# A gated mix of linear attention and a state-space convolution: how the filter taps reach all partitions, and when they are prepared

## The chip, the cores and the metric

The kernel runs on one core of one Trainium2 chip. A core has a matrix engine (TensorE; PE in the profile, its weight loads PEld), a vector engine (VectorE, DVE), a scalar engine (ScalarE, ACT), a general engine (GpSimd, POOL) and a queue engine that mostly issues transfers (SyncE, SP). The metric is the time of one execution on the device in microseconds (us); the profile adds the span, from the first to the last instruction.

## The reference

For one sequence of 2048 positions with 448 channels the reference computes, cut to its core:

```
q, k, v = split(x @ wqkv)                 # 16 heads of 28 channels
phi(t)  = where(t > 0, t + 1, exp(t)) + 1e-6
kv      = sum over s of phi(k)^T v        # per head; not causal
a       = (phi(q) @ kv / (phi(q) . sum phi(k) + 1e-6)) @ wo
K[d, l] = 2 Re sum_n C[d, n] dt[d] exp(A[d, n] dt[d] l)      # filter taps
b       = causal_convolution(x, K) + x * D_skip
g       = sigmoid(sum(x * gate_w))
out     = g * a + (1 - g) * b
```

A is -exp(log_A_real) + i A_imag, C is C_real + i C_imag, dt is exp(log_dt), with 256 modes for each of the 448 channels.

## The kernel before

Positions are cut into 16 chunks of 128 (`NC`, numbered c), channels into 4 groups of 112 (`J`, `DJ`). Products in full precision are made of rounded parts: an operand is split into a high part (a cast on ScalarE) and a low part (the rest, a subtraction on GpSimd or VectorE; `split_t`, `split_n`, `low`), and each product is three rounds of matmuls.

The order of the work is written out by hand, and each engine runs its own instructions strictly in that order. One turn of the main loop (L476, c from 2 to 13) does this:

- SP issues the load of chunk c + 3 (`load_x`, L200).
- TensorE projects the keys of chunk c + 1 (`project` into PSUM tile "k" or "v1", 11 matmuls, L334). ScalarE (L360, L361, then `k_high`, L366) and VectorE (L362, then `k_low`, two times L372) turn them into features.
- TensorE projects the queries of chunk c (`project` into PSUM tile "q", 11 matmuls). `q_post` makes features of them: ScalarE L380 and L349, VectorE L350 and L353. L353 is the last reader of tile "q". PSUM is full: there is one tile "q", one "k", "v0", "v1" and four sums "g".
- TensorE adds the products of features and positions to the four sums (`do_g`, 11 matmuls, L403).
- ScalarE and GpSimd split chunk c + 2 (`split_t`: L240, L236; `split_n`: L246, L236, and `skip`, L252).

The convolution of this input needs only the first tap of each channel, as a running sum over positions times that tap. `do_v` (L410, L411) multiplies by a triangle of ones, `tri`, for chunks 0 and 1 in turn c = 5 and later for the rest; `v_post` (L415, VectorE) multiplies by the row of taps `near`, which has the 448 taps in every partition; the last row of each product goes by two small transfers into `u` (L418, SP), and GpSimd adds the product to `y` (L423). `gcr` is a second constant, used after the loop.

The generator `s4d_prepare` (from L279) makes the taps and tests that the first tap is enough. `steps(n)` lets it run over n of its pieces: the exponentials before the loop; sums over the modes of channel groups 0 and 1 (L290 and L291 on ScalarE, L292 on VectorE) at the end of c = 2, of groups 2 and 3 at the end of c = 3; thirteen small VectorE instructions on 112 partitions x 4 (L280, L281, L299 to L309) at the end of c = 4; then, in c = 5, between the query projection and `do_g`, the four transposes that spread the result `p0`, 112 x 4, over 128 partitions (L313, TensorE) and the copy from PSUM into `near` (L314, ScalarE):

```
o = ps.tile([P, 512], F32, name="p", tag="v1")
for j in range(J):
    PE.transpose(o[:, j * DJ:(j + 1) * DJ], p0[:, j:j + 1].to_broadcast([DJ, P]), ident[:DJ, :DJ])
ACT.copy(near, o[:, :D])
```

At the end of c = 3, behind the L292 of groups 2 and 3, VectorE also casts `tri` (L511) and `gcr` (L512). The parameters of the convolution, `abc`, are four arrays of 448 KB that lie in space of `pq` which chunks 6 to 15 fill later. They are loaded by four transfers, with the load of chunk 4 behind the first (L230, L200). The output weights `wvo`, 1792 KB, are loaded in turn c = 4 (L482) and first read in turn c = 11 (L531). After the loop come the products with the sums, the normalisation and the output chunk by chunk (`turn`, `attend`, `final_b`).

Of the kernel before, what the change touches and what calls it, by code (L numbers as in the profile page):

```python
# [7 lines left out]
F32 = mybir.dt.float32  # L8
# [7 lines left out]
P = 128  # L16
S = 2048
D = 448
# [3 lines left out]
NC = S // P  # L22
J = 4
DJ = D // J
# [116 lines left out]
def gated_mix_kernel(ctx: ExitStack, tc: tile.TileContext, xin, wq_d, wvo_d, abc_d, ldt_d, dsk_d,  # L141
                     turn_d, cst_d, first_d, gin_d, out):
    nc = tc.nc
    PE, ACT, DVE, POOL, SP = nc.tensor, nc.scalar, nc.vector, nc.gpsimd, nc.sync

    keep = ctx.enter_context(tc.tile_pool(name="keep", bufs=1))
    pq = keep.tile([P, NC, D], F32, name="pq")
# [9 lines left out]
    work = ExitStack()  # L157
# [7 lines left out]
    ident, trir = both[:, 0], both[:, 1]  # L165
    cst = const.tile([P, DJ + RX + 1], F32, name="cst")
    mask, gcat, sel = cst[:DJ, :DJ], cst[:UZ, DJ:DJ + RX], cst[:, DJ + RX:]
    gcr = const.tile([UZ, RX], F32R, name="gcr")
    ones = const.tile([P, P], F32R, name="ones")
    rows = const.tile([P, S], F32, name="rows")  # L170
    near, dsk = (rows[:, i * D:(i + 1) * D] for i in range(2))
# [8 lines left out]
    tri = const.tile([P, P], F32R, name="tri")  # L180
# [3 lines left out]
    xn_p = work.enter_context(tc.tile_pool(name="xn", bufs=7))  # L184
    tp = work.enter_context(tc.tile_pool(name="tp", bufs=2))
    ps = work.enter_context(tc.tile_pool(name="ps", bufs=1, space=PSUM))

    warm = tp.tile([P, 512], mybir.dt.bfloat16, name="warm", tag="e")
    POOL.memset(warm, 1.0)
# [7 lines left out]
    def load_x(c):  # L197
        r = xp.tile([P, XC], F32, name="xr", tag="xr")
        turned[c], plain[c] = r[:, :NAT], r[:, NAT:]
        SP.dma_start(out=r, in_=xin[c])  # L200
# [4 lines left out]
    abc = pf[:DJ, 3 * J * N:7 * J * N].rearrange("p (i j n) -> p i j n", i=4, j=J)  # L205
    wkr = {}
    o = 0
    for part in PARTS:
# [8 lines left out]
        o = e  # L217
# [8 lines left out]
    SP.dma_start(out=dsk, in_=dsk_d.to_broadcast([P, D]))  # L226
    load_x(3)
    SP.dma_start(out=ldt, in_=ldt_d)
    for i in range(4):
        SP.dma_start(out=abc[:, i], in_=abc_d[:, i])  # L230
        if i == 0:
            load_x(4)
    SP.dma_start(out=both, in_=turn_d)

    def low(eng, o, r, h):
        eng.tensor_tensor(out=o, in0=r, in1=h.bitcast(F32), op=ALU.subtract)  # L236

    def split_t(c):
        w = xt[c] = xt_p.tile([P, 2 * NAT], F32R, name="xt", tag="t")
        ACT.copy(w[:, :NAT], turned[c])  # L240
        low(POOL, w[:, NAT:], turned[c], w[:, :NAT])

    def split_n(c):
        r, w = plain[c], xn_p.tile([P, NX], F32R, name="xn", tag="n")
        xn[c] = w
        ACT.copy(w[:, :XC - NAT], r)  # L246
        low(POOL, w[:, XC - NAT:], r[:, :D], w[:, :D])
        if c > 2:
            skip(c)

    def skip(c):
        POOL.tensor_tensor(out=y[:, c], in0=plain[c][:, :D], in1=dsk, op=ALU.mult)  # L252
# [22 lines left out]
    def small():  # L275
        cnt[0] += 1
        return sm[:, cnt[0] - 1]

    def s4d_prepare():  # L279
        tt = lambda eng, o, a, b, op: eng.tensor_tensor(out=o, in0=a, in1=b, op=op)  # L280
        stt = lambda o, a, k, b, op1: DVE.scalar_tensor_tensor(out=o, in0=a, scalar=k, in1=b, op0=ALU.mult, op1=op1)  # L281
        junk = [yf[:DJ, F0 + (i - 2) * 2 * N:F0 + (i - 1) * 2 * N].rearrange("p (i n) -> p i n", i=2) for i in range(2)]
        s0, s1, dt, am, p0, p1, d2, md, b0, b1 = (small() for _ in range(10))
        for j in range(J):
            ACT.activation(abc[:, 0, j], abc[:, 0, j], AF.Exp)
        ACT.activation(dt, ldt, AF.Exp)
        tt(DVE, d2, dt, dt, ALU.mult)
        yield
        for j in range(J):
            ACT.activation(junk[0], abc[:, 0:2, j], AF.Square, accum_out=am[:, j:j + 1])  # L290
            ACT.activation(junk[0][:, 0], abc[:, 2, j], AF.Copy, accum_out=s0[:, j:j + 1])  # L291
            DVE.scalar_tensor_tensor(out=junk[1], in0=abc[:, 2:4, j], scalar=1.0, in1=abc[:, 0:2, j], op0=ALU.mult,  # L292
                                     op1=ALU.mult, accum_out=s1[:, j:j + 1])
            if j % 2:
                yield
        tt(DVE, md, am, d2, ALU.mult)
        stt(p0, s0, 2.0, dt, ALU.mult)
        stt(p1, s1, -2.0, d2, ALU.mult)
        DVE.tensor_scalar(out=md, in0=md, scalar1=SMALL, scalar2=None, op0=ALU.is_le)  # L299
        stt(b0, p0, -1.0, p0, ALU.max)  # L300
        stt(b1, p1, -1.0, p1, ALU.max)
        yield
        DVE.tensor_scalar(out=p0, in0=p0, scalar1=-BIG, scalar2=BIG, op0=ALU.max, op1=ALU.min)
        DVE.scalar_tensor_tensor(out=md, in0=b0, scalar=1.0 / FAR, in1=md, op0=ALU.is_ge, op1=ALU.mult)
        stt(okc, b1, FLAT, b0, ALU.is_le)
        DVE.scalar_tensor_tensor(out=md, in0=b0, scalar=FAR, in1=md, op0=ALU.is_le, op1=ALU.mult)
        tt(DVE, okc, okc, md, ALU.mult)
        tt(DVE, p0, p0, okc, ALU.mult)
        DVE.tensor_reduce(out=oks, in_=okc, op=ALU.add, axis=AX.X)  # L309
        yield  # L310
        o = ps.tile([P, 512], F32, name="p", tag="v1")
        for j in range(J):
            PE.transpose(o[:, j * DJ:(j + 1) * DJ], p0[:, j:j + 1].to_broadcast([DJ, P]), ident[:DJ, :DJ])  # L313
        ACT.copy(near, o[:, :D])  # L314

    def pieces(c, wh, wl, n, tag, last=None):
        o = ps.tile([P, 512], F32, name=tag, tag=tag)
# [20 lines left out]
    def project(*args, **kw):  # L338
        o, run = pieces(*args, **kw)
        run(11)  # L340
        return o
# [15 lines left out]
    def k_feature(c, o):  # L357
        e = tp.tile([P, D], F32, name="e", tag="e")
        pks[c] = o[:, :D]
        ACT.activation(e, pks[c], AF.Relu, scale=-1.0)  # L360
        ACT.activation(e, e, AF.Exp, scale=-1.0)  # L361
        DVE.scalar_tensor_tensor(out=pks[c], in0=pks[c], scalar=1.0, in1=e, op0=ALU.add, op1=ALU.max)  # L362

    def k_high(c):
        pkh[c] = tp.tile([P, 512], F32R, name="pkh", tag="pkh")[:, EDGE:EDGE + D]
        ACT.add(pkh[c], pks[c], 1e-6)  # L366
# [41 lines left out]
    def do_v(c):  # L408
        v = vt[c] = ps.tile([P, 512], F32, name="v", tag="v%d" % (c % 2))
        PE.matmul(v[:, :D], lhsT=tri, rhs=xn[c][:, :D], start=True, stop=False)  # L410
        PE.matmul(v[:, :D], lhsT=tri, rhs=xn[c][:, XC - NAT:], start=False, stop=True)  # L411

    def v_post(c):
        t = tp.tile([P, D], F32, name="t", tag="v0")
        DVE.tensor_tensor(out=t, in0=vt.pop(c)[:, :D], in1=near, op=ALU.mult)  # L415
        if c < NC - 1:
            for k in (c, UL + c):
                SP.dma_start(out=u[k:k + 1], in_=t[P - 1:P])  # L418
            v_add(c, t)
        return t  # L420

    def v_add(c, t):
        POOL.tensor_tensor(out=y[:, c], in0=y[:, c], in1=t, op=ALU.add)  # L423

    prep = s4d_prepare()
    def steps(n):
        for _ in range(n):
            next(prep, None)
# [47 lines left out]
    for c in range(2, NC - 2):  # L476
        if c + 3 < NC:
            load_x(c + 3)
        if c == 2:
            SP.dma_start(out=cst, in_=cst_d)  # L480
        if c == 4:
            SP.dma_start(out=wvo, in_=wvo_d)  # L482
        vs = VS.get(c, ())
        ko = project(c + 1, wkh, wkl, D, "v1" if c in (2, 4) else "k")
        for v in vs[:1]:
            do_v(v)
        split_t(c + 2)
        k_feature(c + 1, ko)
        k_high(c + 1)
        if c > 5:  # L490
            for v in vs[:1]:
                v_post(v)
        k_low(c + 1)
        qo = project(c, wqh, wql, D + 2, "q")
        if c == 5:
            steps(1)
        else:
            for v in vs[1:]:
                do_v(v)
        q_post(c, qo)  # L500
        if c == 10:
            split_n(c + 2)
        if c == 5:
            v_post(0)
        else:
            for v in vs[1:]:
                v_post(v)
        if c < 5:
            steps(2 if c == 4 else 1)
        if c == 3:  # L510
            DVE.tensor_copy(tri, trir)  # L511
            DVE.tensor_copy(gcr, gcat)  # L512
        if c == 7:
            SP.dma_start(out=okr[:, None, :DJ], in_=oks[:, None, :])
        if c == 9:
            DVE.tensor_reduce(out=okr[:, DJ:], in_=okr[:, :DJ], op=ALU.add, axis=AX.X)
            DVE.tensor_copy(okn, okr[:, DJ:])
        do_g(c)
        if c == 5:
            do_v(1)  # L520
        if c < 4:
            skip(c - 1)
        if c != 10:
            split_n(c + 2)
        if c == 5:
            v_post(1)
        for j in {11: (0, 1), 12: (2, 3)}.get(c, ()):
            w = xn_p.tile([P, NX], F32R, name="wo", tag="n")[:DJ, :2 * D].rearrange("p (i d) -> p i d", i=2)
            woh.append(w[:, 0])
            wol.append(w[:, 1])  # L530
            ACT.copy(woh[j], wo[:, j])  # L531
            low(POOL, wol[j], wo[:, j], woh[j])
# [109 lines left out]
    c = NC - 2  # L642
# [294 lines left out]
```

## Time and profile before

| | us |
|---|---|
| median of three runs (lowest, highest) | 174.25 (173.95, 174.47) |
| the profiled execution | 174.06 |
| its span | 172.2 |
| TensorE busy in the span | 167.8 |
| VectorE busy | 113.9 |
| ScalarE busy | 96.0 |
| GpSimd busy | 120.0 |

How to read it: a busy share is an average over the whole span. A group's row names the line, the engine, the operation, what it writes and reads, and its size; then how many there were. In the timeline a row begins with its start and its duration in us, and what stands in brackets is the idle time of that engine just before it and whose work ended that. Successive instructions overlap a little, so a row may start before the row ahead of it has ended. SPq rows are issues of transfers: the transfer itself lands later. The slices of the page cut the span into 40 equal parts of 4.3 us.

### The profile page before, as it was taken

What the parts mean: (1) busy time and instruction counts of PE and PEld (TensorE: products, weight loads), DVE (VectorE), ACT (ScalarE), POOL (GpSimd) and SP (SyncE); (2) the same over time, 40 slices, a digit from 0 to 9 for tenths busy, and PEclk for the clock granted to TensorE, in tenths of its full rate; (3) what the DMA queues carried; (4) which work ended last, traced back from release to release, by engine and by line L of the source; (5) the groups of instructions that cost most, each with busy time, mean ns of one, the idle gap of its engine ahead of it and who ended that gap; (6) DMA issues with size and microseconds to landing.
All of it is one profiled execution on the core that took longest, in us unless ns stands there. A gap on an engine that the chain in (4) does not pass through costs nothing. (4 is left out here: it accounts for less than half of the span.)

```text
span 172.2 us, 2796 instructions
## 1 busy us (share of the span) xinstructions
PE 167.8 (97%) x876; PEld 152.0 (88%) x876; DVE 113.9 (66%) x240; ACT 96.0 (56%) x221; POOL 120.0 (70%) x128
## 2 busy tenths in 40 slices
PE   6999999999999999999999999999999999999992
PEld 2788999999899999999999999999899999999992
DVE  0847737698975483846627346487898998987542
ACT  3688588894256262542727456356574564664541
POOL 6082667877529988696996999529968998892200
PEclk9999999999999999999999999999999999999999
DMA  5989975097003031230404200000031222122213
GB/s 173 415 297 294 268 209 166 0 368 303 4 0 114 11 123 34 95 123 1 122 15 131 106 1 1 0 0 2 7 67 54 107 89 76 62 99 107 108 59 108
DMA packets 7962, 18.60 MB, mean 108 GB/s; under 512 B 2045, under 2 KB 4810, under 8 KB 7818
## 3 DMA queue, kind: packets, MB, share of 16 engines
q1 hardware_dynamic: 7802, 18.30, 32.0%
q8 instruction: 7, 0.11, 0.3%
q10 hardware_dynamic: 144, 0.11, 0.2%
q14 instruction: 9, 0.07, 0.1%
HBM read 14.38 MB, written 3.67 MB: 105 GB/s over the span
## 5 line engine op out<-in xcount | busy, mean ns | idle before, releaser
L629 PE MATMUL a<-wk,th 128*128 128x448 f32 (+1 forms) x170 | 36.4, 360 | 0.0
L403 PE MATMUL g<-pkh,xn 128*128 128x448 f32 x112 | 35.6, 364 | 0.0
L629 PEld LDWEIGHTS a<-wk,th 128*128 128x128 f32 x170 | 29.5, 189 | 1.6
L334 PE MATMUL k<-wk,xt 128*128 128x448 f32 x132 | 29.3, 367 | 0.0
L334 PE MATMUL q<-wqh,xt 128*128 128x450 f32 x120 | 27.5, 366 | 0.0
L362 DVE SCALAR_TENSOR_TENSOR k<-k,e 128x448 f32<-128x448 f32 x12 | 7.6, 632 | 29.4 <-ACT e L361 29.4
L423 POOL TENSOR_TENSOR y<-y,t 128x448 f32<-128x448 f32 x16 | 18.7, 1168 | 11.5 <-DVE t L415 11.5
L334 PEld LDWEIGHTS k<-wk,xt 128*128 128x128 f32 x132 | 24.8, 189 | 2.2 <-DVE wk L236 0.3
L334 PEld LDWEIGHTS q<-wqh,xt 128*128 128x128 f32 x120 | 22.5, 188 | 1.7
L236 POOL TENSOR_TENSOR xn<-xr,xn 128x448 fp32r<-128x448 f32 x16 | 19.4, 1211 | 6.6 <-ACT xn L246 4.5
L403 PE MATMUL g<-pkl,xn 128*128 128x448 f32 x64 | 23.4, 366 | 0.0
L403 PEld LDWEIGHTS g<-pkh,xn 128*128 128x128 f32 x112 | 21.0, 188 | 2.2
L236 POOL TENSOR_TENSOR xt<-xr,xt 128x512 fp32r<-128x512 f32 x14 | 18.2, 1297 | 5.9 <-ACT xt L240 5.9
L360 ACT ACTIVATE e<-k 128x448 f32<-128x448 f32 x12 | 6.5, 544 | 26.9 <-PE k L334 26.9
L542 POOL TENSOR_TENSOR prod<-pq,zb 128x448 f32<-128x448 f32 x16 | 18.6, 1172 | 4.1 <-ACT zb L665 3.0
L252 POOL TENSOR_TENSOR y<-xr,rows 128x448 f32<-128x448 f32 x16 | 18.8, 1175 | 0.0
L567 POOL TENSOR_TENSOR pn<-pq,den 128x336 f32<-128x336 f32 x16 | 12.3, 771 | 5.9 <-ACT den L556 4.1
L634 DVE SCALAR_TENSOR_TENSOR ot<-y,og,a 128x448 f32<-128x448 f32 (+1 forms) x17 | 10.7, 629 | 5.1 <-PE a L629 5.1
L612 DVE TENSOR_TENSOR th<-tr,th 128x512 fp32r<-128x512 f32 x16 | 11.0, 691 | 2.7 <-ACT th L611 2.1
L403 PEld LDWEIGHTS g<-pkl,xn 128*128 128x128 f32 x64 | 11.2, 174 | 1.2 <-DVE pkl L372 0.2
L611 ACT CAST th<-tr 128x512 fp32r<-128x512 f32 x16 | 9.4, 588 | 4.6 <-PE tr L604 4.4
L334 PE MATMUL q<-wql,xt 128*128 128x450 f32 x45 | 11.6, 364 | 0.0
(150 smaller groups left out, 302.3 us busy)
## 6 DMA issues: line engine op xcount, KB each, us to landing
xr<-in SPq DMA_DIRECT2D x15, 512.0 KB, 6.2
out<-ot SPq DMA_DIRECT2D x15, 224.0 KB, 1.9
pq<-in SPq DMA_DIRECT2D x4, 448.0 KB
wvo<-in SPq DMA_DIRECT2D x1, 1792.0 KB
y<-in SPq DMA_DIRECT2D x2, 480.0 KB
y<-in SPq DMA_DIRECT2D x2, 450.0 KB
u<-t SPq DMA_DIRECT2D x30, 1.8 KB, 1.7
y<-in SPq DMA_DIRECT2D x1, 448.0 KB, 4.3
```

The lines of the kernel that those rows point to most:

```text
L236: eng.tensor_tensor(out=o, in0=r, in1=h.bitcast(F32), op=ALU.subtract)
L252: POOL.tensor_tensor(out=y[:, c], in0=plain[c][:, :D], in1=dsk, op=ALU.mult)
L334: PE.matmul(o[:, :n], lhsT=a, rhs=b, start=run.n == 1, stop=not seq)
L362: DVE.scalar_tensor_tensor(out=pks[c], in0=pks[c], scalar=1.0, in1=e, op0=ALU.add, op1=ALU.max)
L403: PE.matmul(g[i][:a.shape[1], :D], lhsT=a, rhs=b, start=c == 0 and n == 0, stop=c == NC - 1 and n == len(seq) - 1)
L423: POOL.tensor_tensor(out=y[:, c], in0=y[:, c], in1=t, op=ALU.add)
L542: POOL.tensor_tensor(out=pd[c], in0=pq[:, c], in1=zb, op=ALU.mult)
L567: POOL.tensor_tensor(out=n[:, :3, :DJ].rearrange("p j (h d) -> p j h d", h=4), in0=a, in1=r[:, :H - 4].rearrange("p (j h) -> p j h", j=3)[ ...
L611: ACT.copy(h, ov)
L612: DVE.tensor_tensor(out=l, in0=ov, in1=h.bitcast(F32), op=ALU.subtract)
L629: PE.matmul(a[:, lo:hi], lhsT=u_, rhs=w_[:, lo:hi], start=n == 0, stop=n == 10)
L634: DVE.scalar_tensor_tensor(out=ot[:, lo:hi], in0=y[:, c, lo:hi], scalar=og[:, c:c + 1], in1=a[:, lo:hi], op0=ALU.mult, op1=ALU.add)
```

## The change

- The four transposes and the PSUM tile "p" go. In their place SP writes `p0` into a DRAM row `nd` of 448 values, one piece of four values (16 bytes) for each of 112 partitions, and reads this row back into all 128 partitions, into the last chunk's place in `pq`. ScalarE copies it from there into `near`, putting the order (r, j) into (j, r).
- The small instructions of the preparation move from the end of c = 4 to the end of c = 3 (`steps(3)`). The two transfers of the taps are issued in c = 5, behind the load of chunk 8.
- The casts of `tri` and `gcr` move from VectorE at the end of c = 3 to ScalarE at the end of c = 4.
- `near` and `v_post(0)` now stand behind `do_g(5)` and `split_n(7)` in c = 5, ahead of `v_post(1)`.
- The load of `wvo` moves from c = 4 to c = 5, behind the two transfers of the taps.
- The four arrays `abc` are loaded by two transfers of two arrays each, with the load of chunk 4 between them.

```
+    nd = work.enter_context(tc.tile_pool(name="nd", bufs=1, space=bass.MemoryType.DRAM)).tile([1, D], F32, name="nd")
...
-    for i in range(4):
-        SP.dma_start(out=abc[:, i], in_=abc_d[:, i])
-        if i == 0:
-            load_x(4)
+    SP.dma_start(out=abc[:, :2], in_=abc_d[:, :2])
+    load_x(4)
+    SP.dma_start(out=abc[:, 2:], in_=abc_d[:, 2:])
...
-        yield
-        o = ps.tile([P, 512], F32, name="p", tag="v1")
-        for j in range(J):
-            PE.transpose(o[:, j * DJ:(j + 1) * DJ], p0[:, j:j + 1].to_broadcast([DJ, P]), ident[:DJ, :DJ])
-        ACT.copy(near, o[:, :D])
...
-        if c == 4:
+        if c == 5:
+            SP.dma_start(out=nd.rearrange("o (r j) -> (o r) j", j=J), in_=p0)
+            SP.dma_start(out=pq[:, NC - 1], in_=nd.to_broadcast([P, D]))
             SP.dma_start(out=wvo, in_=wvo_d)
...
-        if c == 5:
-            steps(1)
-        else:
+        if c != 5:
             for v in vs[1:]:
                 do_v(v)
         q_post(c, qo)
...
-        if c == 5:
-            v_post(0)
-        else:
+        if c != 5:
             for v in vs[1:]:
                 v_post(v)
-        if c < 5:
-            steps(2 if c == 4 else 1)
-        if c == 3:
-            DVE.tensor_copy(tri, trir)
-            DVE.tensor_copy(gcr, gcat)
+        if c < 4:
+            steps(3 if c == 3 else 1)
...
+        if c == 4:
+            ACT.copy(tri, trir)
+            ACT.copy(gcr, gcat)
         if c == 5:
+            ACT.copy(near.rearrange("p (j r) -> p j r", j=J), pq[:, NC - 1].rearrange("p (r j) -> p j r", j=J))
+            v_post(0)
             v_post(1)
```

More of the change, by code (lines that the diff above doesn't have):

```diff
@@ L282, in s4d_prepare @@
         junk = [yf[:DJ, F0 + (i - 2) * 2 * N:F0 + (i - 1) * 2 * N].rearrange("p (i n) -> p i n", i=2) for i in range(2)]
-        s0, s1, dt, am, p0, p1, d2, md, b0, b1 = (small() for _ in range(10))
+        s0, s1, dt, am, p1, d2, md, b0, b1 = (small() for _ in range(9))
         for j in range(J):
@@ L423, in v_add @@
         POOL.tensor_tensor(out=y[:, c], in0=y[:, c], in1=t, op=ALU.add)
+    p0 = small()
     prep = s4d_prepare()
```

## The prediction

> **What bounds the kernel now.** I read the page's busy shares and slices first, then the waits of TensorE's weight loads, then the timeline of each engine from 36 to 50 us, where the moved work stands.
>
> ```profile
> PE 167.8 (97%) x876; PEld 152.0 (88%) x876; DVE 113.9 (66%) x240; ACT 96.0 (56%) x221; POOL 120.0 (70%) x128
> ...
> PEclk9999999999999999999999999999999999999999
> ...
> GB/s 173 415 297 294 268 209 166 0 368 303 4 0 114 11 123 34 95 123 1 122 15 131 106 1 1 0 0 2 7 67 54 107 89 76 62 99 107 108 59 108
> ```
> ```profile
> PEld p L313 <- DVE sm L280: 0.2, 1, 0.2
> ```
>
> TensorE is busy 97% of the span, its clock is full in every slice, and the one wait of its loads in the stretch that the edit touches is 0.2 us. So the kernel is a stream of matmuls one behind another; the edit is worth what it takes out of that stream, less every wait that it puts in. Other engines count only where they make the stream wait. The sum is made against the profiled execution, 174.06 us with a span of 172.2 us; the median of the runs, 174.25 us, lies 0.19 us above it.
>
> **What leaves TensorE.** The four transposes of the taps:
>
> ```profile
> 45.84 0.59 PEld L334 LDWEIGHTS q<-wql,xt 128*128 128x128 f32 x3
> 46.66 0.38 PEld L313 LDWEIGHTS p<-both,sm 112*128 112x128 f32 x4 [0.23 <-DVE sm L280]
> 47.00 0.19 PEld L403 LDWEIGHTS g<-pkh,xn 128*128 128x128 f32 x1
> ```
>
> The projection q(5) ends its loads at 45.84 + 0.59 = 46.43, and do_g(5) begins at 47.00. Without the transposes it begins at 46.43: **-0.57 us** (0.34 us of work, 0.23 us of waiting for the prep).
>
> **What moves on VectorE.** This term decides. The thirteen small prep instructions of c = 4 now stand at the end of c = 3, behind the last two L292, where the casts tri and gcr stood; the casts go to ScalarE. The rows of before, with GpSimd's of the same time:
>
> ```profile
> 37.43 1.17 DVE L511 CAST tri<-both 128x128 fp32r<-128x128 f32 x1
> 38.52 1.18 DVE L512 CAST gcr<-cst 128x112 fp32r<-128x112 f32 x1
> 39.63 0.62 DVE L362 SCALAR_TENSOR_TENSOR v<-v,e 128x448 f32<-128x448 f32 x1
> ```
> ```profile
> 41.93 1.38 DVE L350 TENSOR_SCALAR t<-e 128x448 f32<-128x448 f32 x1
> 43.42 0.62 DVE L353 SCALAR_TENSOR_TENSOR pq<-q,t 128x448 f32<-128x448 f32 x1
> 43.96 0.38 DVE L280 TENSOR_TENSOR sm<-sm 112x4 f32<-112x4 f32 x1
> 44.27 1.33 DVE L281 SCALAR_TENSOR_TENSOR sm<-sm 112x4 f32<-112x4 f32 x2
> 45.52 0.16 DVE L299 TENSOR_SCALAR sm<-sm 112x4 f32<-112x4 f32 x1
> ...
> 46.59 0.62 DVE L362 SCALAR_TENSOR_TENSOR k<-k,e 128x448 f32<-128x448 f32 x1
> ```
> ```profile
> 37.15 1.36 POOL L236 TENSOR_TENSOR xn<-xr,xn 128x448 fp32r<-128x448 f32 x1 [0.93 <-ACT xn L246]
> 38.48 1.15 POOL L252 TENSOR_TENSOR y<-xr,rows 128x448 f32<-128x448 f32 x1
> 39.59 1.28 POOL L236 TENSOR_TENSOR xt<-xr,xt 128x512 fp32r<-128x512 f32 x1
> 41.90 1.16 POOL L236 TENSOR_TENSOR xn<-xr,xn 128x448 fp32r<-128x448 f32 x1 [1.03 <-ACT xn L246]
> 43.02 1.30 POOL L252 TENSOR_TENSOR y<-xr,rows 128x448 f32<-128x448 f32 x1
> 44.28 1.29 POOL L236 TENSOR_TENSOR xt<-xr,xt 128x512 fp32r<-128x512 f32 x1
> ```
> ```profile
> L281 DVE SCALAR_TENSOR_TENSOR sm<-sm x4: 150/150/1254, 44.3 to 45.7; 112x4 f32<-112x4 f32 x4
> ```
>
> The ends tell why a cast takes 1.17 us. GpSimd's instructions end at 37.15 + 1.36 = 38.51 and 38.48 + 1.15 = 39.63; tri ends at 38.60 and gcr at 39.70, each just behind the GpSimd instruction that ran when it came. The small prep instructions do the same: L280 ends at 44.34 with GpSimd's L252 (44.32), and the first L281, 0.15 us by the median, takes 1.254 us, until GpSimd's next instruction is over. So a VectorE instruction with both ends in SBUF waits out the running GpSimd instruction, and where GpSimd's follow back to back, one passes at each boundary. L362 and L353, which read PSUM, take 0.62 us beside anything.
>
> The Trainium skill states this as a rule in "SBUF — State Buffer", section "Who interferes with whom": a VectorE instruction with two SBUF inputs, or in a mode of two ports, and a GpSimd instruction that reads SBUF shut each other out for a whole instruction. The trace agrees (1.254 us against 0.150 us). The rule speaks against this change: by it the sum is the one below, without it rival 1.
>
> Now the thirteen behind the last L292. GpSimd's rows from 37.15 to 40.87 depend on nothing that the edit moves. The first prep instruction (L280) comes at 37.43 and passes at 38.51; the first L281 passes at 39.63; the second at the end of GpSimd's third, 39.59 + 1.28 = 40.87, or, like its twin (ended 44.27 + 1.25 = 45.52 where GpSimd's ended 45.57), at 40.82. GpSimd then idles until ScalarE's next xn, which is itself behind this chain. The other ten ran freely in before, from L299's start (45.52) to L362's (46.59): 1.07 us. A row starts some 0.08 us before the last one's end (L353 ends 44.04, L280 starts 43.96). So k(5)'s L362 starts at 40.82 - 0.08 + 1.07 = 41.81. It stood at 39.63: **2.18 us later**. The other bound: unheld at 1.07 / 10 us each, thirteen end at 38.8, ahead of where L362 stood, which is no delay. I take the first, since the same instructions met the same GpSimd instructions at 44 us.
>
> **Who waits for that.** ScalarE stands in order behind L362: k_high's L366, q_post(4)'s L380 and L349, split_n(6)'s L246.
>
> ```profile
> 40.28 0.55 ACT L366 ACTIVATE pkh<-v 128x448 fp32r<-128x448 f32 x1 [1.52 <-DVE v L362]
> ...
> 41.19 0.63 ACT L246 CAST xn<-xr 128x512 fp32r<-128x512 f32 x1
> ```
> ```profile
> 44.27 0.55 ACT L360 ACTIVATE e<-k 128x448 f32<-128x448 f32 x1 [1.93 <-PE k L334]
> ```
>
> All of it, and GpSimd's xn behind L246, shifts by the same 2.18 us, so L350 again meets that xn (they started at 41.93 and 41.90) and again takes 1.38 us. L353 of q(4) then ends at 43.42 + 0.62 + 2.18 = 46.22. It is the last reader of the one PSUM tile "q", which q(5) has to write:
>
> ```profile
> 44.22 1.61 PEld L334 LDWEIGHTS q<-wqh,xt 128*128 128x128 f32 x8
> ```
>
> In before, L353 ended at 44.04 and q(5) began at 44.22: 0.18 us to spare. For the signal I take 0.06 us (the transposes began at 46.66, when VectorE had turned from the prep to L362 at 46.59). So q(5) begins at 46.28, and the stream stands still for **+2.06 us**. Behind q(5) are queued do_g(5), do_v(1) and k(7), all on TensorE; as TensorE stays the bound to the end, nothing gives it back.
>
> **The rest of the edit, costed at nothing, with its cover.**
>
> ```profile
> 50.56 2.51 SPq L418 DMA_DIRECT2D u<-t  x4
> ```
> ```profile
> DMA to landing us min/median/max: 1.6/1.7/2.4
> ```
> ```profile
> out<-ot SPq DMA_DIRECT2D x15, 224.0 KB, 1.9
> ```
> ```profile
> L531 ACT CAST wo<-wvo x4: 578/579/580, 92.9 to 100.4; 112x448 fp32r<-112x448 f32 x4
> ```
> ```profile
> 8.35 0.35 SPq L200 DMA_DIRECT2D xr<-in  x1
> ```
> ```profile
> 24.43 0.62 ACT L240 CAST xt<-xr 128x512 fp32r<-128x512 f32 x1
> ```
> ```profile
> DMA to landing us min/median/max: 3.6/6.2/10.9
> ```
>
> tri and gcr on ScalarE, 128 and 112 columns: at most the 0.63 us of L246's 512 columns each, at least nothing; 1.26 us fit into ScalarE's 1.93 us of idle time before L360. With the delay, L246 ends at 44.00 and tri by 44.63, while do_v(0), its first reader, would run ahead of q(5) at 43.8. That wait of 0.8 us or less lies inside the 2.06 us (two matmuls of 0.2 us still end before 46.28). If nothing is late, tri is there by 42.5.
>
> The taps by DMA: p0 is ready at about 41.8. SP issues the 16-byte pieces (0.63 us an issue, by the four u), waits for them (1.6 to 2.4 us, by the 1.8 KB u rows), and issues the broadcast of 224 KB, for which I take the same 1.6 to 2.4 us (stores of that size land in 1.9): there at 46.3 to 47.9. ScalarE reaches the near copy behind q(5)'s L349 and split_n(7): q(5) ends at 46.28 + 11 loads of 0.2 = 48.5, and L380, L349 and L246 took 1.0 us from L366's end (40.83 to 41.82), so near starts at 49.6 with 1.7 us or more in hand. Without that cover, near would hold v_post(0) and (1) and, through PSUM tile v0, do_v(2), which comes after do_g(5), do_v(1) and k(7), at 53.3. near's strided read may take 0.63 us or twice that; near and v_post(0), the latter 0.6 us like L353, are over by 51.5. So the DMAs can be some 3.5 us late before TensorE feels it.
>
> SP's queue: nd, the broadcast and wvo now stand between load_x(8) and the u rows; while SP waits for p0, nothing else is due. wvo, 1792 KB, goes out at about 45.5 and takes 5 to 6 us at the 368 to 303 GB/s of its slices in before; its first reader is at 92.9. The u rows come at about 50.9 instead of 50.56, and load_x(9) behind them as before, 0.4 us later, while its reader moves by 1.5 us.
>
> Two parameter loads for four: load_x(4), issued at 8.35, gets another 448 KB ahead of it, 1.7 us at the 268 GB/s of the fifth slice. At the slowest landing of an xr (10.9 us) it is there at 21.0, and first read at 24.43. The PSUM tile "p" that goes had no other user waiting.
>
> **Sum**: -0.57 + 2.06 = **+1.49 us**: 175.55 us against the profiled 174.06, or 175.74 against the median. I say 175.7.
>
> **Rivals** (times against the median).
> 1. The prep hides (faster). If the thirteen pass GpSimd unheld, only the transposes count: 174.25 - 0.57 = 173.7 us. It decides at L362's delay: up to 0.12 us (0.18 less 0.06) the full gain stands, and up to 0.69 us the edit is no loss. For it: instructions of four columns are so short that several might slip through one boundary. Against it: the very same L280 and L281 did not, at 44.3.
> 2. Half a stall. Had L350 come ahead of the xn by the 0.03 us between their starts, it would need only what it ran after xn's end (43.31 less 43.06 = 0.25 us) instead of 1.38: +0.36 us, 174.6. If two boundaries hold and not three, 1.24 us less: 174.5. For it: the small margin. Against it: both starts follow L366 at fixed distances (1.65 and 1.62 us).
> 3. The stall costs the clock.
>
> ```profile
> 1.33 4.21 PE L258 MATMUL q<-warm 128*128 128x512 bf16 x10 [1.33 <-POOL warm L189]
> ```
>
> These first matmuls, 512 columns each, take 0.42 us apiece, twice the pace of the loop (0.20 us for 448). If 2 us of silence brought that pace back for 4.2 us, 2.1 us are added: 177.8. Against it: the granted clock is full throughout, though no gap in the loop tests it. The Trainium skill ("TensorE: Matmul & The Clock Gate", section "What's actually happening") asks for about 3.4 us of idleness; no run here shows that.
> 4. The DMA chain is more than 3.5 us late: 176 to 178, by how late.
>
> **How the numbers follow.** Forecast 0.68, rival 1 0.17, rival 2 0.08, rivals 3 and 4 together 0.07. The forecast's own range is 175.2 to 176.2: 0.5 us either way, as far as the runs of before lie apart. The whole range reaches down to rival 1, 173.5, and up to 176.5, a stall half longer than computed. No change means within 0.3%, 0.52 us, about what a measurement of this kernel can tell: rival 1 lies just beyond that, so it gives 0.12 to faster and 0.05 to same; rival 2 gives 0.07 to same and 0.01 to slower.
>
> **What would show it.** Right: three prep instructions of about 1.1 us behind the last L292, L362 of k(5) near 41.8, TensorE waiting about 2 us for L353 ahead of q(5), and no other new wait. Wrong: the thirteen over by 39, or q(5) at 44.2; ScalarE waiting for the broadcast ahead of near; a granted clock below full after 46.

## The result: 1.2% slower

The changed kernel takes 176.02 us (median; 175.87 to 176.54), the kernel before 174.02 us beside it: ratio 1.0118, 95% interval 1.0098 to 1.0137, 2.00 us more. 175.7 us was forecast against a median of 174.25 us, that is +1.5 us. The profiled execution has a span of 174.6 us (172.2 before).

TensorE's weight loads name the new wait (the view of waits of the changed kernel: who waited for whom, us in total, times, the longest):

```profile
PEld q L329 <- DVE pq L348: 1.7, 1, 1.7
PEld v L405 <- ACT tri L517: 0.4, 1, 0.4
```

The changed lines are numbered lower: L329 is the projection (L334 before), L348 the last reader of the query tile (L353), L345 is L350, L357 is L362, L405 is the first load of do_v. VectorE's timeline of the changed kernel shows how the wait came about:

```profile
37.91 1.10 DVE L280 TENSOR_TENSOR sm<-sm 112x4 f32<-112x4 f32 x1
38.93 1.19 DVE L281 SCALAR_TENSOR_TENSOR sm<-sm 112x4 f32<-112x4 f32 x2
40.04 0.16 DVE L299 TENSOR_SCALAR sm<-sm 112x4 f32<-112x4 f32 x1
40.12 1.34 DVE L281 SCALAR_TENSOR_TENSOR sm<-sm 112x4 f32<-112x4 f32 x2
...
42.22 0.62 DVE L357 SCALAR_TENSOR_TENSOR v<-v,e 128x448 f32<-128x448 f32 x1
...
44.53 1.36 DVE L345 TENSOR_SCALAR t<-e 128x448 f32<-128x448 f32 x1
46.00 0.62 DVE L348 SCALAR_TENSOR_TENSOR pq<-q,t 128x448 f32<-128x448 f32 x1
```

GpSimd's timeline of the same stretch, and VectorE's L281 there (shortest, median and longest in ns) with the first of them alone:

```profile
37.64 1.35 POOL L236 TENSOR_TENSOR xn<-xr,xn 128x448 fp32r<-128x448 f32 x1 [0.94 <-ACT xn L246]
38.95 1.15 POOL L252 TENSOR_TENSOR y<-xr,rows 128x448 f32<-128x448 f32 x1
40.06 1.30 POOL L236 TENSOR_TENSOR xt<-xr,xt 128x512 fp32r<-128x512 f32 x1
```
```profile
L281 DVE SCALAR_TENSOR_TENSOR sm<-sm x4: 149/634/1268, 38.9 to 41.3; 112x4 f32<-112x4 f32 x4
```
```profile
38.93 0.15 DVE L281 SCALAR_TENSOR_TENSOR sm<-sm 112x4 f32<-112x4 f32 x1
```

Three prep instructions are held, 1.1 to 1.3 us each, until a GpSimd instruction ends: L280, and the second and the third L281. The first L281 passes at the end of the same GpSimd instruction as L280, in 0.15 us. L357 comes at 42.22 where it came at 39.63. The stream of weight loads follows (the changed kernel, TensorE's loads):

```profile
42.09 2.19 PEld L329 LDWEIGHTS k<-wk,xt 128*128 128x128 f32 x11
44.67 0.19 PEld L405 LDWEIGHTS v<-xn,tri 128*128 128x128 f32 x1 [0.40 <-ACT tri L517]
...
46.67 1.54 PEld L329 LDWEIGHTS q<-wqh,xt 128*128 128x128 f32 x8 [1.71 <-DVE pq L348]
...
48.82 0.19 PEld L398 LDWEIGHTS g<-pkh,xn 128*128 128x128 f32 x1
...
51.43 2.20 PEld L329 LDWEIGHTS k<-wk,xt 128*128 128x128 f32 x11
```

The first and the last of these rows, k(6) and k(7), in the kernel before:

```profile
41.62 2.19 PEld L334 LDWEIGHTS k<-wk,xt 128*128 128x128 f32 x11
```
```profile
49.53 2.21 PEld L334 LDWEIGHTS k<-wk,xt 128*128 128x128 f32 x11
```

So the profiled execution was 0.47 us late ahead of the moved work (42.09 against 41.62). Free of that, q(5) comes 46.67 - 44.22 - 0.47 = 1.98 us late, and k(7) 51.43 - 49.53 - 0.47 = 1.43 us: the stall costs 1.98 us, and what the transposes took, 0.55 us, comes off. From then on no wait on TensorE is new. The rest stands at the end of the program. ScalarE's last row, of the kernel before and of the changed one:

```profile
170.03 0.59 ACT L640 COPY pq<-a 128x224 f32<-128x224 f32 x2 [2.05 <-DVEq L847]
```
```profile
171.90 0.59 ACT L636 COPY pq<-a 128x224 f32<-128x224 f32 x2 [2.05 <-DVE ot L630]
```

From its end to the end of the span (172.23 and 174.55 us) pass 1.61 us before and 2.06 us after. That 0.45 us was not in the forecast.

### The profile page after: what moved, and what is told of

It reads as the page before. It is cut to its first block, busy times and chain, and to the rows that moved or that the text cites. A ratio compares the mean times of both kernels' runs of the same rounds, so it can differ in the third digit from the quotient of the medians.

```text
span 174.6 us, 2785 instructions
## 1 busy us (share of the span) xinstructions
PE 168.3 (96%) x872; PEld 151.8 (87%) x872; DVE 111.6 (64%) x238; ACT 96.9 (56%) x223; POOL 120.0 (69%) x128
## 5 line engine op out<-in xcount | busy, mean ns | idle before, releaser
L329 PE MATMUL k<-wk,xt 128*128 128x448 f32 x132 | 29.9, 372 | 0.0
L329 PE MATMUL q<-wqh,xt 128*128 128x450 f32 x120 | 27.6, 367 | 1.3 <-DVE pq L348 1.3
L357 DVE SCALAR_TENSOR_TENSOR k<-k,e 128x448 f32<-128x448 f32 x12 | 7.6, 632 | 32.0 <-ACT e L356 32.0
L329 PEld LDWEIGHTS k<-wk,xt 128*128 128x128 f32 x132 | 25.0, 190 | 2.2 <-ACT wk L429 0.4
L329 PEld LDWEIGHTS q<-wqh,xt 128*128 128x128 f32 x120 | 22.5, 188 | 3.5 <-DVE pq L348 1.7
L329 PE MATMUL q<-wql,xt 128*128 128x450 f32 x45 | 11.6, 363 | 0.0
```

Source lines behind the costliest of these rows:

```text
L329: PE.matmul(o[:, :n], lhsT=a, rhs=b, start=run.n == 1, stop=not seq)
```

## The experiments

In the summary, "ahead" is how late k(6) is against the kernel before, in the profiled execution; "loop" is what the same matmul, behind the edit, about the 70th us of the kernel before, is late beyond that; "end" is the stretch from ScalarE's last row to the end of the span (1.61 us before). All in us; "before" is the median beside it.

| run | median | before | ratio (95%) | ahead | loop | end |
|---|---|---|---|---|---|---|
| changed kernel | 176.02 | 174.02 | 1.0118 (1.0098 to 1.0137) | +0.47 | +1.43 | 2.06 |
| changed kernel again | 176.27 | 173.92 | 1.0141 (1.0119 to 1.0162) | -0.21 | +1.43 | 2.26 |
| early prep alone | 175.95 | 173.92 | 1.0116 (1.0096 to 1.0135) | +0.30 | +1.81 | 1.61 |
| prep reads PSUM | 175.69 | 173.92 | 1.0109 (1.0089 to 1.0128) | -0.17 | +1.28 | 2.06 |
| one boundary less | 175.16 | 173.82 | 1.0079 (1.0056 to 1.0103) | -0.15 | +0.46 | 2.09 |
| late prep | 178.67 | 173.92 | 1.0238 (1.0178 to 1.0297) | +0.23 | +3.84 | 2.06 |
| late prep, weights early | 175.86 | 173.82 | 1.0123 (1.0105 to 1.0140) | -0.19 | +1.07 | 2.28 |
| and later products | 174.19 | 173.94 | 1.0014 (1.0002 to 1.0025) | -0.19 | -0.44 | 2.27 |
| and the row in SBUF | 182.00 | 174.19 | 1.0438 (1.0415 to 1.0462) | -0.20 | +7.50 | 2.31 |
| row without a reader | 174.75 | 173.94 | 1.0054 (1.0030 to 1.0078) | -0.17 | 0.00 | 2.38 |
| two loads alone | 174.36 | 173.82 | 1.0031 (1.0015 to 1.0046) | +0.15 | +0.21 | 1.73 |
| casts alone | 174.53 | 173.82 | 1.0039 (1.0025 to 1.0053) | -0.24 | -0.08 | 1.61 |

The theory was the prediction's: GpSimd holds the prep, the prep delays L362, and through the one query tile that stops TensorE. The rivals were the route through DRAM, the later weights, and the casts.

**The changed kernel again.**

> The changed kernel once more. 175.9 to 176.2 us. The first half us of its profile's delay lay ahead of the eighth us, in the landing of the first parameters, which the edit does not touch: if it is chance, the profile now differs there from the first by some tenths of a us; if it belongs to the edit, it comes again with 0.4 to 0.5 us.

The median lies just above the expected range. The loop's +1.43 us came again to the hundredth; what lies ahead of the edit was -0.21 instead of +0.47 us, so it is not the edit's. Over all runs it goes from -0.24 to +0.47, and it goes with the start of the clock: the trace's record of the granted clock begins, at full, at 6.95 us in the first profile of this kernel and at 4.73 in the second, and the four runs in which it begins after 6.3 us are the four that are 0.15 us or more late. The price of the edit in these profiles is therefore 1.43 us in the loop and 0.45 to 0.65 us at the end, 1.9 to 2.1 us. The medians say 2.00 and, with four executions, 2.35.

**The early prep alone**, added to the kernel before:

```
-            steps(2 if c == 4 else 1)
-        if c == 3:
-            DVE.tensor_copy(tri, trir)
-            DVE.tensor_copy(gcr, gcat)
+            steps({3: 3, 4: 0}.get(c, 1))
...
+        if c == 4:
+            ACT.copy(tri, trir)
+            ACT.copy(gcr, gcat)
```

> The kernel before with the prep moved to c = 3 and the two casts on ScalarE, nothing else: the transposes, the weights and the loads stay. Theory: the stall of 2.06 us ahead of q(5) is here too, and of the transposes' 0.57 us only the waiting (0.23 us) is saved: 174.02 + 1.83 = 175.85 us. Rival (the DMA route costs the time): 173.8 to 174.0.

175.95 us, 0.10 us from the theory's number, and the loop is 1.81 us longer where 1.83 had been forecast. TensorE's loads of this run show the same stall with no DMA route in the kernel:

```profile
46.49 1.52 PEld L334 LDWEIGHTS q<-wqh,xt 128*128 128x128 f32 x8 [1.70 <-DVE pq L353]
48.03 0.59 PEld L334 LDWEIGHTS q<-wql,xt 128*128 128x128 f32 x3
48.63 0.53 PEld L313 LDWEIGHTS p<-both,sm 112*128 112x128 f32 x4
49.11 0.19 PEld L403 LDWEIGHTS g<-pkh,xn 128*128 128x128 f32 x1
```

The transposes follow q(5) without a wait, and still 0.49 us pass from q(5)'s last load (48.62) to do_g(5). So nearly all of the 0.57 us is the transposes themselves; the prediction had 0.34 of work and 0.23 of waiting. Its profile also holds an extra 0.34 us near 122 us, between the two products with the output weights, which the run with the casts alone has too. No run explains it, and with it the closeness of the median is in part luck.

**One GpSimd instruction less among the three**, in the changed kernel:

```
-        if c > 2:
+        if c > 2 and c != 5:
             skip(c)
...
         if c == 4:
+            skip(5)
             ACT.copy(tri, trir)
```

> The changed kernel with one GpSimd instruction (skip of chunk 5, L252) moved from the middle of the three that hold the prep to the end of c = 4. Theory (each GpSimd instruction in a row holds one prep instruction): one boundary less, L362's twin for k(5) 1.1 us earlier, the wait ahead of q(5) about 1 us instead of 2: 174.9 to 175.2 us. Rival (the delay of the prep is its own length, or comes from ScalarE or the transfers): no change, 176.0 to 176.3.

175.16 us. VectorE's and GpSimd's timelines of this run:

```profile
37.30 1.11 DVE L280 TENSOR_TENSOR sm<-sm 112x4 f32<-112x4 f32 x1
38.33 1.33 DVE L281 SCALAR_TENSOR_TENSOR sm<-sm 112x4 f32<-112x4 f32 x2
39.58 0.16 DVE L299 TENSOR_SCALAR sm<-sm 112x4 f32<-112x4 f32 x1
39.65 0.23 DVE L281 SCALAR_TENSOR_TENSOR sm<-sm 112x4 f32<-112x4 f32 x2
...
40.65 0.62 DVE L357 SCALAR_TENSOR_TENSOR v<-v,e 128x448 f32<-128x448 f32 x1
```
```profile
37.02 1.37 POOL L236 TENSOR_TENSOR xn<-xr,xn 128x448 fp32r<-128x448 f32 x1 [0.93 <-ACT xn L246]
38.35 1.29 POOL L236 TENSOR_TENSOR xt<-xr,xt 128x512 fp32r<-128x512 f32 x1
```

Two GpSimd instructions in a row hold two prep instructions, the rest runs free. L357 is 40.65 - 39.63 + 0.15 = 1.17 us late instead of 2.12 (42.22 - 39.63 - 0.47), and the loop gives back 0.97 us. Delay and price fall together, one for one, as the theory has it; the rival's "no change" fails.

**The prep's scratch values in PSUM**, in the changed kernel (the core of it):

```
+        scr = ps.tile([P, 512], F32, name="scr", tag="v0")[:DJ]
+        dq, d2, mq, q0, p1, b0, oq = (scr[:, i * J:(i + 1) * J] for i in range(7))
...
-        tt(DVE, md, am, d2, ALU.mult)
-        stt(p0, s0, 2.0, dt, ALU.mult)
+        tt(DVE, mq, d2, am, ALU.mult)
+        stt(q0, dq, 2.0, s0, ALU.mult)
```

> The changed kernel with one difference: the scratch values of the thirteen small prep instructions lie in a PSUM tile (tag v0, free at that time), so that each reads at most one operand from SBUF; two small copies are added. Theory (the prep waits for GpSimd's instructions, that delays the last reader of the query tile, TensorE stands still): none of the prep instructions takes over 0.3 us at the end of c = 3, L362's twin starts near 39 us, q(5) does not wait, and only the saved transposes count: 173.4 to 173.6 us, 0.5 us under the kernel before. Rival (the route through DRAM, the later output weights or the moved casts cost the time): 175.5 to 176, as the changed kernel.

That no prep instruction is long came true, the time did not: 175.69 us, which is the rival's number, though not by the rival's cause. VectorE's timeline of this run:

```profile
34.80 1.40 DVE L352 TENSOR_SCALAR t<-e 128x448 f32<-128x448 f32 x1
...
37.56 1.52 DVE L297 SCALAR_TENSOR_TENSOR y<-pq 112x512 f32<-112x512 f32 x1
...
39.01 0.16 DVE L280 TENSOR_TENSOR scr<-scr,sm 112x4 f32<-112x4 f32 x1
39.28 0.38 DVE L281 SCALAR_TENSOR_TENSOR scr<-scr,sm 112x4 f32<-112x4 f32 x2
...
41.43 0.62 DVE L364 SCALAR_TENSOR_TENSOR v<-v,e 128x448 f32<-128x448 f32 x1
```

No prep instruction is held any more (0.15 to 0.17 us each). But the queries' L352, 0.47 us in the changed kernel at this place, now met a GpSimd instruction and took 1.40; so the second of the sums (L297 here, L292 before) came later, was held in turn (1.52 us instead of 0.69), and the fifteen instructions in PSUM, each waiting for the one before, took 2.4 us. L364 starts 41.43 - 39.63 + 0.17 = 1.97 us late, q(5) waits 1.71 us for the last reader of the query tile, as in the changed kernel, and the loop pays accordingly. The hold moved to other instructions; the delay of L362, by whatever cause, is what TensorE pays for.

**The DMA route with the prep at its old place**, in the changed kernel:

```
-        if c < 4:
-            steps(3 if c == 3 else 1)
+        if c < 5:
+            steps(2 if c == 4 else 1)
```

> The changed kernel with the prep at its old place, the end of c = 4. Theory: no stall ahead of q(5); the taps are ready near 45.7 us and their broadcast lands near 49.6, 1 to 2 us after ScalarE wants it, which is about all the cover there is ahead of do_v(2): 0 to 0.5 us of new waiting, so 173.5 to 174.0 us. Rival (the two transfers take much longer than 1.4 and 2 us, or hold ScalarE's queue so that a projection waits): 174.5 to 176.

178.67 us: missed, and the reason is the broadcast. The stall ahead of q(5) is gone. SP's issues of the taps, the broadcast and the weights, and ScalarE's near copy, which waited:

```profile
46.03 0.33 SPq L478 DMA_DIRECT2D nd<-sm  x1
47.42 0.33 SPq L479 DMA_DIRECT2D pq<-nd  x1
47.80 0.42 SPq L480 DMA_DIRECT2D wvo<-in  x1
```
```profile
52.71 0.98 ACT L520 COPY rows<-pq 128x448 f32<-128x448 f32 x1 [4.52 <-DMA pq<-nd]
```

5.3 us pass from issue to the copy, where 1.6 to 2.4 had been taken from other transfers. do_v(2) waited 2.92 us, and the clock went with it (a row of TensorE's loads, then windows of the same run: length; busy us and instructions of TensorE, its loads, VectorE, ScalarE and GpSimd; the granted clock, the DMA share and GB/s):

```profile
54.40 0.29 PEld L405 LDWEIGHTS v<-xn,tri 128*128 128x128 f32 x1 [2.92 <-DVE t L410]
```
```profile
52.00:54.00 2.00, 0.00 (x0) 0.00 (x0) 0.28 (x1) 1.29 (x2) 0.00 (x0) 1.00 1.01 429
54.00:56.00 2.00, 1.60 (x4) 1.48 (x5) 1.51 (x3) 1.27 (x4) 1.51 (x2) 0.56 0.94 402
56.00:58.00 2.00, 2.00 (x7) 1.77 (x7) 0.56 (x2) 0.50 (x1) 1.98 (x2) 0.58 0.06 10
58.00:60.00 2.00, 2.00 (x11) 1.86 (x11) 1.56 (x5) 1.11 (x3) 1.16 (x1) 1.00 0.76 261
```

The clock is half for 3.4 us (2 us at 0.56 and 2 at 0.58 make (0.44 + 0.42) x 2 / 0.5), and seven matmuls pass in 2 us instead of eleven: 1.7 us more. By windows of 1 us the last matmul ahead of the wait ends at 51.85 and the clock falls at 54.26, after 2.4 us without a matmul. One of the four timed executions took 176.47 us, 2.2 under the median; its granted clock is 1.00 and that of the others 0.99, so it went without that loss. It was not the profiled one, so how long its wait was is not known.

**The same with the weights ahead of the taps** (`wvo` in c = 4, where it was before the edit):

> The changed kernel with the prep at its old place and the output weights loaded in c = 4 again, ahead of the taps' transfers. In the run with the late prep the broadcast took 5.3 us from issue to the near copy, with the weights' 1792 KB issued 0.4 us behind it. Theory (the weights' traffic shares the transfer engines with the broadcast): alone it lands within 1.6 to 2.4 us, near starts by 50 us, do_v(2) does not wait, and the loop is 0.5 us shorter than before; with 0.45 us more at the end of the program 173.8 to 174.0 us. Rival (a broadcast out of one DRAM row takes 5 us by itself): do_v(2) waits 2.5 to 3 us as before, 176.5 to 179.

175.86 us, between theory and rival. The broadcast was issued at 47.01; the near copy:

```profile
51.03 0.97 ACT L521 COPY rows<-pq 128x448 f32<-128x448 f32 x1 [3.25 <-DMA pq<-nd]
```

That is 4.0 us with no other large transfer beside it (4.1 in the next run). So the weights cost about 1.3 us of the 5.3; the greater part is the broadcast's own. do_v(2) waited 1.7 us, and here the clock stayed full.

**And with the second product later** (do_v(2) and v_post(2) behind q(6)):

```
-        for v in vs[:1]:
+        for v in vs[:1] if c != 6 else ():
             do_v(v)
...
-            for v in vs[1:]:
+            for v in vs[c != 6:]:
                 do_v(v)
```

> The run with the late prep and the early weights, with one thing more: do_v(2) and v_post(2) stand behind the query projection of c = 6, beside do_v(3), instead of ahead of it, about 2.3 us later. The broadcast landed 4.0 us after its issue there and do_v(2) waited 1.7 us. Theory (the stream then waits for nothing new): the loop is 0.48 us shorter than the kernel before, the end of the program 0.45 to 0.67 us longer, as in each kernel with the DRAM row: 173.7 to 174.1 us, no gain to speak of. If the end did not lengthen: 173.3.

174.19 us against 173.94, ratio 1.0014, 0.1 us above the range. The loop is 0.44 us shorter than before, no wait takes its place, and the end of the program, 0.66 us longer, eats it: no gain, as forecast.

**The row and its transfers without a reader**, added to the kernel before:

```
+        if c == 5:
+            SP.dma_start(out=nd.rearrange("o (r j) -> (o r) j", j=J), in_=p0)
+            SP.dma_start(out=pq[:, NC - 1], in_=nd.to_broadcast([P, D]))
```

> The kernel before with the DRAM row and its two transfers added in c = 5; nothing reads what they bring, the taps still go by the transposes. If the row and its transfers cost the end of the program, 3.58 us or more pass from the last matmul to the span's end instead of 3.13, and the time is 0.45 us over the kernel before: 174.2 to 174.5. If the longer end comes from another part of the edit, 173.8 to 174.0.

174.75 us, more than the 174.2 to 174.5 that were forecast. In the loop nothing moves (0.00), the end grows to 2.38 us: the two transfers alone cost the end of the program 0.77 us in this profile. The page's line on instruction loading counts 9 transfers in each kernel without the two (the kernel before, early prep, two loads, casts) and 10 in each with them, as here:

```profile
q14 instruction: 10, 0.08, 0.1%
```

The traces hold one thing more. Among the last instructions of SP, in each of the eight kernels with the two transfers, there is one stretch of about 0.4 us in which SP does nothing, for no cause that the trace names; the four without them have no such stretch. That is most of the 0.45 us of the changed kernel. That SP then waits for the tenth load fits, but no run takes the load away by itself, so this stays open.

**The row in SBUF** (`nd = pq[:1, NC - 2]`, on top of the run with the later products):

> The run with the late prep and the later products, with the row of taps in one partition of SBUF (a free place in pq) instead of DRAM. It tells what the DRAM tile does from what two more transfers do. If the longer end belongs to the DRAM tile, the last stretch is short again (1.61 us from ScalarE's last row to the span's end, as in the kernel before) and the time is 173.3 us, 0.5 under the kernel before. If it belongs to the two transfers, 173.8 to 174.1. Against both: 128 reads of one partition may take longer than the 4.0 us of the reads from DRAM; from about 6 us on the stream waits for the second product with the taps, and the time is above 174.2.

182.00 us. The end stays long (2.31 us, 10 instruction loads), so the longer end belongs to the two transfers and not to the DRAM tile. And the broadcast out of one partition, issued at 47.62, was there only for a copy at 57.58, after 10.0 us; TensorE waited 6.0 us, and its granted clock was half for 6.8 us around the end of that wait. The copy:

```profile
57.58 0.98 ACT L521 COPY rows<-pq 128x448 f32<-128x448 f32 x1 [9.81 <-DMA pq<-pq]
```

**Two loads alone** (the `abc` lines of the diff in the kernel before):

> The kernel before with the four parameter loads made two, nothing else. Prediction's account: nothing, 173.7 to 174.3 us; chunk 4 lands 1.5 to 3 us later than at 19.3 us and is still there before it is read at 24.4. For the end of the program: from the last matmul's end to the span's end pass 3.13 us in the kernel before and 3.58 or more in each kernel that has the DRAM row. If it is the row that costs it, 3.13 stays here; if it is any change of SP's program, it moves.

174.36 us, 0.3% over the kernel before (0.15% to 0.46%): not the nothing that was forecast. In its profile the end is 0.12 us longer, and VectorE stands idle for 0.51 us ahead of L352, the last reader of the query tile, for no cause that the profile names, so that q(5) waits 0.37 us. Whether that recurs in every execution stays open; 0.2 us of loop and 0.1 of end are about all that one execution shows of the 0.5.

**The casts alone** (the `tri` and `gcr` lines of the diff in the kernel before):

> The kernel before with the two casts on ScalarE at the end of c = 4, nothing else. Theory (VectorE's waits for GpSimd set when k(5)'s L362 starts): without the casts it starts with its operand, 0.8 to 0.9 us earlier, the prep ends 0.6 us earlier, and the transposes' wait of 0.23 us goes: 173.6 to 173.8 us. Rival (the casts cost ScalarE's chain as much): 173.9 to 174.2.

174.53 us: above the theory's range and the rival's. VectorE does what the theory says (L362 starts at 38.55, which is 39.63 - 0.24 - 38.55 = 0.84 us early; the prep ends 0.8 us early), but the loop gains only 0.08 us: the transposes had hardly waited, as the run with the early prep showed too; and near 120 us the gap of the run with the early prep alone comes again, which makes the rest 0.36 us later. That is +0.28 us of the 0.7 us that the medians show; the rest stays open.

## Why the prediction was right, point by point

- **What bounds.** Right: what the loop lost or won shows as a wait of TensorE, a piece of its work or its clock.
- **Transposes, -0.57 us.** -0.55 measured, but the parts were wrong: 0.49 us is what the transposes take without a wait, and not 0.34.
- **Thirteen instructions behind L292, L362 2.18 us late.** Measured 2.12. Three boundaries held three instructions, but not the three named: L280, the second L281 and the third L281. The prediction misread its own row: in the kernel before, too, it was the second L281 that took 1.254 us, while the first (44.27, 0.15 us) passed together with L280. "One passes at each boundary" is therefore wrong; here the held one passes and a short one with it (the first L281 at the first boundary, L299 at the second). The delay came out all the same, since the instructions still met all three boundaries, and the number of these sets it.
- **Stall +2.06 us.** Measured 1.98. L345 met GpSimd's xn again and took 1.36 us, so the small margin that rival 2 names was not crossed.
- **do_v(0) waits for tri, 0.8 us or less, inside the stall.** 0.40 us, inside it.
- **Rival 1** (the prep hides) fell with the three held rows; **rival 3** (the clock) did not occur in the changed kernel, whose clock is full in the loop, yet it is real: after a wait of 2.92 us in the run with the late prep.
- **The taps' transfers.** The step's sizes were wrong. The pieces landed in 1.4 us (1.6 to 2.4 taken), the broadcast took 4.0 to 5.3 us (1.6 to 2.4 taken), since stores and small rows had stood in for a broadcast. It cost the loop nothing only because p0 was early: issued at 43.66, the broadcast was there by 47.7 to 49.0 (an estimate by those 4.0 to 5.3 us), and near started at 50.22, directly behind split_n(7). In the kernel with the late prep the same mistake decided the time.
- **Chunk 4.** "There at 21.0" was too early: the slowest landing of an xr grew from 10.9 to 13.7 us, issued at 8.77, so 22.5. It still comes ahead of its reader.
- **near's copy** took 1.01 us, inside 0.63 to twice that.
- **The sum, +1.49 us against 2.00.** The loop's part was +1.43, and the mechanism is the one forecast. What failed is an omission: the sum held nothing for the end of the program, where the two added transfers cost 0.45 to 0.65 us in the changed kernel. "Cost nothing" had been argued for their place in the loop alone. The time forecast, 175.7 us, came within 0.32 us of 176.02 in part by luck: the kernel before ran 0.23 us faster beside the changed one (174.02) than in the runs that the forecast set out from (174.25).

```profile
DMA to landing us min/median/max: 3.2/8.5/13.7
```

This is the row of the changed kernel's chunk loads on which the point on chunk 4 rests. The first two L281 of the kernel before, one by one, on which the point on the thirteen instructions rests:

```profile
44.27 0.15 DVE L281 SCALAR_TENSOR_TENSOR sm<-sm 112x4 f32<-112x4 f32 x1
```
```profile
44.34 1.25 DVE L281 SCALAR_TENSOR_TENSOR sm<-sm 112x4 f32<-112x4 f32 x1
```

The Trainium skill's rule on the shared port ("SBUF — State Buffer", section "Who interferes with whom") is borne out by the held rows and by the free ones of the run in PSUM. Its clock rule ("TensorE: Matmul & The Clock Gate", section "What's actually happening") asks for a window of about 3.4 us of idleness. In the profiled execution with the late prep a wait of 2.92 us was enough, so the measurement decides.

## What to carry to other kernels

Before small VectorE work is moved to an earlier place, count the GpSimd instructions that run back to back there: each can hold one instruction for up to its whole length, however short the held one is. The question is then what stands behind it on VectorE and which PSUM tile that has to free. Price a broadcast by a measured broadcast and not by a store of the same bytes, and price an added transfer at the end of the program too. An earlier place for a producer is worth something only if its consumer was late.

## What the runs showed of the hardware that was not expected

- The broadcast of one row of 1792 bytes to 128 partitions took 4.0 us from issue to use out of DRAM and 10.0 us out of one SBUF partition; stores of the same 224 KB land in 1.9 us.
- A wait of 2.92 us of TensorE's loads was followed by half clock for 3.4 us, in the profiled execution and, by the granted clock, in three of four. Waits of 1.7 us, the changed kernel's and that of the run with the early weights, left the clock full.
- A short VectorE instruction can pass a GpSimd boundary together with a held one: the first L281 took 0.15 us right behind the 1.10 us of L280, and the next 1.1 us again.
- The two added transfers lengthened the end of the program by 0.45 to 0.77 us in each of the eight kernels that had them (one profile each, two of the changed kernel).
